# Delta rule and gated feed-forward on one core: joining the first chunk's inverses unit by unit, and the second chunk's on TensorE

## The chip, the cores and the metric

The kernel runs on one NeuronCore of a Trainium2 chip. The metric is device microseconds of one execution. Engines are named as in the profile: PE is TensorE (PEld its weight loads), DVE VectorE, ACT ScalarE, POOL GpSimd, SP the queue of SyncE that issues most transfers.

## The reference

Four batches of eight heads, 768 steps, head size 48. Per head a state S (48 x 48) is carried along the steps, with normalized keys:

```python
for t in range(S):
    y[:, :, t] = q_t @ state
    v_old = k_t @ state
    state = state + beta_t * outer(k_t, v_t - v_old)
x = y.transpose(0, 2, 1, 3).reshape(3072, 384)
h = x @ w_in                                  # 384 -> 2048
out = (h / (1 + exp(-1.702 * h))) @ w_out     # 2048 -> 384
```

The two weight matrices come as float64 and are turned into float32 on the chip.

## The kernel before

**Chunks and units.** The 768 steps are cut into six chunks of 128. A unit is one chunk of one batch with its eight heads; there are 24, in order n = 0 to 23, four to a chunk (B = 4). From chunk 1 on, a unit holds half a chunk (64 steps) of two batches (class `Half`). Within a chunk the recurrence is solved as a triangular system: the Gram matrix G of the keys, its 32 x 32 diagonal blocks inverted (`invert`, L647), and then, block by block, U = inverse x V (`solve`), with what U does to later rows subtracted from V (`below`).

**Inverting.** `invert` works on VectorE, 128 small systems side by side on the partitions, in steps that each are a multiply (P) and a reduce. It inverts the two 16 x 16 halves of every block; where the chunk is not the first, ten further pairs, five to make A = N10 x Y0 and five to make the corner from it (the loops over `(j, Q)` and `(i, Q)`), join the halves to the inverse of the 32 x 32 block. The result goes through DRAM (Yd) into XBs, where `inverse[n]` lies. For chunk 0 the join is made on TensorE by `merge` (L734): psP = G x (right columns of the inverse), scaled by `upper` on ScalarE, then psZ = inverse (transposed on VectorE) x that, added to the columns by a product with the identity. As a generator it makes psP of both units, then psZ of both.

**The start.** VectorE converts the weights by bit operations (`conversions`, six steps a piece, the second a ScalarE Relu). These steps stand in the generator `background` (L370), and `fill(us)` takes as many of them as fit an estimate; so the place of a `fill` in the program is the place of the work in VectorE's order. `background` puts the inversion of chunk 1 after the first eight pieces of w_out. TensorE's order is the program's own, since all calls are recorded in order (`pinned`). The stages:

1. Keys normalized, Gram matrices, `invert(0)`, scores of units 0 to 2.
2. The first scan, units 0 and 1: `hops` (L1455) gives eight hops that alternate between the two units, each a list of blocks to solve and a list of blocks whose U is passed on; `together` (L1289) emits one hop: head by head a solve of one unit and all updates of the other (psU, psV), then ScalarE's copies of U and of the next block's V. Between hops stand dummy products (`warm`, ps_warm), transposes of the next chunk's keys (`turn`, psT), two Gram matrices, and `fill(2.1)`. `roots_second` normalizes the next chunk's keys with a root on GpSimd; `paced` holds loads of w_in until a hop is reached.
3. `put_out` of both units: outputs psY, copied to xT, moved between partitions by transfers (xT<-last).
4. The second scan, units 2 and 3, with pieces of the first feed-forward (`feed`, ph) between hops; Gram matrices of units 6 and 7, whose diagonal blocks go by DRAM (Nd) into NT, VectorE's input for chunk 1's inversion.
5. 25 rounds of `fill(1.0)` and `feed`, in which units 8 to 11 are prepared (roots on GpSimd, rn on VectorE, KN scaled on ScalarE) and unit 4's scores are made.

**The slots** (`slot`, L1337, n = 3 to 23). Slot n solves the last block of unit n and the first of unit n + 1 (psU), makes outputs of unit n (four), updates (psR), makes scores of unit n + 2 (four again) and the Gram matrix of n + 6 (psG). Between these, `spend` takes feed-forward pieces (ph, po) from `queue`: 10.5 us of them in slots 3 to 5, 19.5 in later ones, by their estimated cost (1.3 a piece). For what is taken, `spend` also moves the inversion of the units after next along (`inverting`, from slot 4 on for units 8 and 9), and at an even slot the rest of that inversion is put out at once. `follow` adds a pair's feed-forward to the queue after each odd slot from 5 on; until then the queue holds the rest of the first two (`both_written`, `written`). When the queue is empty, `spend` does nothing.

Of the kernel before, what the change touches and what calls it, by code (L numbers as in the profile page):

```python
# [9 lines left out]
I32 = mybir.dt.int32  # L10
# [8 lines left out]
def kernel(  # L19
# [492 lines left out]
    def gram_halves(n):  # L512
# [14 lines left out]
        for t, o in evict:  # L527
# [3 lines left out]
            )  # L531
        ready[n] = KN[n % len(KN)], kT, G
        return G

# [112 lines left out]
    def invert(c, b0=0, nb=B):  # L647
# [86 lines left out]
    def merge(pair, area, banks):  # L734
# [7 lines left out]
        for X, t in zip(Z, XT):  # L742
            vec.transpose(t.rearrange("p h k -> p (h k)"), X.rearrange("p h k -> p (h k)"))
        for X, x, m in zip(pair, Z, Pm):
            ps = banks[0][0].tile([128, H, HS], F32, tag=banks[0][1], name="psP")
# [7 lines left out]
            yield  # L753
        for x, t, m in zip(Z, XT, Pm):
            ps = banks[1][0].tile([128, H, HS], F32, tag=banks[1][1], name="psZ")
            pe.matmul(ps, lhsT=ident, rhs=x[:, :, HS:], start=True, stop=True, skip_group_check=True)
            for h in range(H):
                for r in rows:
# [3 lines left out]
                    )  # L762
            act.copy(x[:, :, HS:], ps)
            yield

# [8 lines left out]
    class Step:  # L774
# [63 lines left out]
        def gather(self):  # L838
# [4 lines left out]
            )  # L843

        def below(self, blk, h, psR):
            r = slice(blk * BS, (blk + 1) * BS)
            for k in range(blk + 1, NB):
                u = slice(k * BS, (k + 1) * BS)
                pe.matmul(
                    self.psV[u, h, :], lhsT=self.G[r, h, u], rhs=self.U[r, h, :],  # L850
                    start=False, stop=True, skip_group_check=True,
                )
# [436 lines left out]
    def together(solves, belows):  # L1289
# [115 lines left out]
    for b in range(B - 1):  # L1405
# [6 lines left out]
        upper, ident.rearrange("p (k o i) -> p k o i", k=NB, o=2)[:, :, 0], axis=AX.XY, op=ALU.add  # L1412
    )
    turn(0)
    for b in range(B):
# [29 lines left out]
    warm(NY // 2)  # L1445
    scaling = roots_second(areas)
    next(scaling)

# [22 lines left out]
    scored = pair[-1].scored  # L1471
    for _ in range(HB):
        next(products)
        next(scored)
        warm(NM // 2)
    next(products)
    paced(inverse[0][0:1, 0, BS // 2 : BS // 2 + 1], 2, 1)
    fill(3.0)
    next(scaling)
    warm(NM)  # L1480
    Nds = []
    for i in range(2 * NB):
        together(*next(path))
# [3 lines left out]
        if i == 0:  # L1487
            warm(NM // 2)
            run(products)
            run(scored)  # L1490
            run(scaling)
        if i == 1:
            for X in pair[:2]:
                X.select()
        if i == 3:
            for b in range(HB, B):
# [7 lines left out]
        if i == 6:  # L1504
            Nds.append(send_blocks(B))
        if i > 5:
            fetch_out(i - 6, other_queue)
        fill(2.1 if i else 1.0)
    put_out(pair[0])
    merging = merge(pair[2:], area, ((ps_big, "big"), (ps_big, "big")))  # L1510
    fill(2.0)
    put_out(pair[1])
    Nds.append(send_blocks(B + 1))
    fetch_out(2, other_queue)
    for X in pair[2:]:
        next(merging)
        X.gather()
        warm(NM // 4)
    fill(4.0)
    for at in range(B):  # L1520
# [22 lines left out]
    for i in range(2 * NB):  # L1543
        if i == 0:
            for _ in range(HB):
                next(merging)
# [5 lines left out]
        if i == 1:  # L1552
            Nds.append(send_blocks(B + HB))
        if i == 2:
            load_diagonals(Nds + [send_blocks(B + HB + 1)])
# [104 lines left out]
```

## Time and profile before

| | us |
|---|---|
| three runs | 690.48, 691.98, 686.99 (median 690.48) |
| profiled execution | 683.09 |
| its span | 681.4 |
| busy TensorE | 660.4 (97%, dummy products included) |
| busy VectorE | 479.5 (70%) |
| busy ScalarE, GpSimd | 233.6 and 269.4 |
| mean granted clock | 0.991 |

Stages of the profiled execution, from the instructions in order of time:

| stage | us from the start |
|---|---|
| first psP (join of unit 0) | 38.7 |
| hops of the first scan | 45.5, 49.1, 51.8, 53.8, 56.1, 58.3, 60.5, 63.3 |
| last output product of unit 1 | ends 69.1 |
| first ph | 77.2 |
| second scan | 78.7 to 96.3, last psY ends 103.0 |
| chunk 1's inversion on VectorE (NT to NT) | 103.1 to 134.3 |
| po begins | 143.3 |
| slots 3, 4, 5, 6, 7 (their psU) | 153.8, 168.8, 184.4, 198.7, 224.8 |

A profile row of TensorE counts instructions; a float32 product is two. The recorded duration of a product includes its way through the array, so start times tell its pace.

### The profile page before, as it was taken

The numbers are of one execution on the slowest core, as the hardware profiler recorded it, in microseconds if no ns is written. First come the engines' busy times: TensorE is split into PE (matmuls) and PEld (weight loads), VectorE is DVE, ScalarE is ACT, GpSimd is POOL, SyncE is SP. The second block draws the span as 40 slices with busy tenths as digits, with TensorE's granted clock in tenths as the row PEclk, the third lists the DMA queues.
The fourth block names the chain that finished last, engine by engine and source line by source line (L and its number), as shares of the span: only waits on it lengthen the run. The fifth ranks groups of instructions, "written<-read, shape, count | busy, mean of one in ns | idle before, by whom it ended". The sixth has DMA issues, their size and how long they took to land.

```text
span 681.4 us, 21731 instructions
## 1 busy us (share of the span) xinstructions
PE 660.4 (97%) x9290; PEld 563.4 (83%) x9290; DVE 479.5 (70%) x890; ACT 233.6 (34%) x571; POOL 269.4 (40%) x282
## 2 busy tenths in 40 slices
PE   9899899799999999999999999999999999999997
PEld 4766678566678998998998988988988988989997
DVE  4889799983788997996997996997976970200000
ACT  2558463632333233333333233233233233322120
POOL 4032844320286634635535526426305205105041
PEclk9799999989999999999999999999999999999999
DMA  9567575263334435335335244244231130100101
GB/s 174 105 165 175 128 218 99 44 155 81 83 74 92 96 63 109 79 67 104 71 67 116 67 90 88 66 86 79 62 78 19 38 75 2 30 2 6 26 0 24
DMA packets 149632, 54.61 MB, mean 80 GB/s; under 512 B 137824, under 2 KB 142656, under 8 KB 149536
## 3 DMA queue, kind: packets, MB, share of 16 engines
q1 hardware_dynamic: 146368, 46.62, 32.7%
q0 software_dynamic: 3168, 6.61, 3.7%
q8 instruction: 73, 1.20, 0.8%
q14 instruction: 23, 0.19, 0.1%
HBM read 38.37 MB, written 13.63 MB: 76 GB/s over the span
## 4 chain that ended last, share of the span: by engine, by line
PE 86%; DVE 6%; ACT 2%; DMA 2%; issue 2%; SPq 1%; DVEq 0%; ACTq 0%
PE po L139 34%; PE ph L139 32%; PE four L139 7%; PE psU L139 3%; PE psR L139 2%; PE psG L139 2%; DVE P L139 2%; DVE w_out L139 2%; PE ps_warm L139 1%; DVE YB L139 1%; DMA TW<-in_q_dram 1%; PE psQ L139 1%; SPq L139 1%; PE psV L139 1%; DVE NT L139 1%
## 5 line engine op out<-in xcount | busy, mean ns | idle before, releaser
L139 PE MATMUL ph<-xT,w_in 128*128 128x256 f32 x1152 | 261.0, 384 | 2.3 <-ACT gT L139 2.0
L139 PEld LDWEIGHTS ph<-xT,w_in 128*128 128x128 f32 x1152 | 215.9, 190 | 33.8 <-ACT gT L139 2.4
L1118 POOL TENSOR_TENSOR gT<-gT 128x512 f32<-128x512 f32 x80 | 103.0, 1298 | 97.9 <-ACT gT L139 66.0
L139 PE MATMUL po<-w_out,gT 128*128 128x192 f32 (+1 forms) x720 | 138.4, 347 | 0.0
L139 DVE TENSOR_TENSOR P<-NT,YB 64x8 f32<-64x8 f32 (+13 forms) x195 | 124.8, 640 | 5.8
L139 PEld LDWEIGHTS po<-w_out,gT 128*128 128x128 f32 x720 | 118.5, 190 | 11.0 <-ACT o L139 0.5
L139 ACT ACTIVATE gT<-ph 128x512 f32<-128x512 f32 x90 | 53.8, 598 | 154.8 <-PE ph L139 154.8
L139 DVE TENSOR_REDUCE YB<-P 64x4 f32<-64x8 f32 (+13 forms) x195 | 78.4, 402 | 6.7
L139 PE MATMUL po<-TW,gT 128*128 128x192 f32 x480 | 81.8, 328 | 0.0
L139 PEld LDWEIGHTS po<-TW,gT 128*128 128x128 f32 x480 | 78.1, 190 | 0.7
L984 POOL TENSOR_SCALAR_AFFINE_SELECT M<-M 64x512 f32<-64x512 f32 x40 | 29.1, 727 | 90.0 <-ACT M L139 88.8
L139 DVE TENSOR_TENSOR o<-o,late 128x192 f32<-128x192 f32 x20 | 6.6, 356 | 68.1 <-ACT late L139 67.9
L139 ACT COPY VU<-psU 32x384 f32<-32x384 f32 x96 | 45.2, 470 | 21.3 <-PE psU L139 14.9
L139 DVE TENSOR_TENSOR VU<-VU,psR 32x384 f32<-32x384 f32 x40 | 22.1, 553 | 36.6 <-PE psR L139 35.9
L400 POOL TENSOR_TENSOR rn<-ssq,half 128x8 f32<-128x8 f32 x12 | 22.3, 1858 | 52.6 <-DVE ssq L139 52.6
L139 DVE TENSOR_TENSOR VU<-VU,four 128x384 f32<-128x384 f32 x19 | 10.4, 548 | 46.1 <-ACT M L139 46.0
L109 POOL DMA_DIRECT2D KN<-in_k_dram x24 | 17.2, 716 | 58.4 <-PE four L139 56.7
L139 ACT COPY o<-po 128x192 f32<-128x192 f32 (+1 forms) x44 | 14.7, 334 | 74.6 <-PE po L139 72.5
L139 PEld LDWEIGHTS psU<-VU,XBs 32*32 32x32 f32 x1536 | 27.4, 105 | 13.5 <-issue 8.5
L139 PE MATMUL psU<-VU,XBs 32*32 32x48 f32 x1536 | 32.6, 203 | 0.3 <-ACT VU L139 0.2
L139 DVE TENSOR_TENSOR P<-NT 64x512 f32<-64x512 f32 (+7 forms) x45 | 30.5, 679 | 1.1
L139 DVE TENSOR_REDUCE NT<-P 64x32 f32<-64x512 f32 (+9 forms) x45 | 30.0, 668 | 1.5
(167 smaller groups left out, 752.1 us busy)
## 6 DMA issues: line engine op xcount, KB each, us to landing
VU<-in_v_dram SPq DMA_DIRECT2D x40, 96.0 KB, 2.8
out_dram<-o SPq DMA_DIRECT2D x40, 96.0 KB, 2.2
QW<-in_q_dram SPq DMA_DIRECT2D x76, 48.0 KB, 2.2
Kd<-KN SPq DMA_DIRECT2D x56, 64.0 KB, 2.2
late<-Kd SPq DMA_DIRECT2D x14, 256.0 KB, 2.8
KN<-in_k_dram POOLq DMA_DIRECT2D x30, 96.0 KB, 3.1
w_out<-in_moe_w_out_dram SPq DMA_DIRECT2D x7, 384.0 KB, 3.8
NT<-Nd SPq DMA_DIRECT2D x20, 128.0 KB, 2.7
```

The lines of the kernel that those rows point to most:

```text
L109: dma(out=place(dst, n)[rows, :, 0:D], in_=src[b, :, t, :].rearrange("h p d -> p h d"),)
L139: return lambda *a, **kw: tc.keep_in_program_order(op(*a, **kw))
L400: nc.gpsimd.tensor_tensor(rn, ssq, half, op=ALU.pow)
L984: nc.gpsimd.affine_select(out=M, in_=M, compare_op=ALU.is_gt, fill=0.0, base=0, pattern=[[0, H], [1, CH]], channel_multiplier=-1,)
L1118: (engine or nc.gpsimd).tensor_tensor(o, a, b, op=op)
```

## The change

It has four parts.

- *The first joins.* `merge` makes psP and psZ of one unit, then of the other. The first hop follows the first unit's join. The second pair's join is spread over hops 5 to 7 of the first scan and the place after the outputs. The scores' second half, the root's continuation, the transposes and the dummy products take other places, `fill` asks for 1.9 instead of 2.1, and the Gram matrices of units 4 and 5 with the sends of all four units move from the first scan and its end into the second scan; three w_out loads on GpSimd's queue move behind the outputs.
- *The scan of units 0 to 3.* `together` emits all eight solves, the copy of U, all eight updates of the next block, the copy of V, and then the updates of the blocks further down, now one product over their joint columns.
- *Chunk 1's join.* The ten pairs on VectorE are made only for c > 1. Units 4 to 7 are joined by the new `merge_halves` with the kept Gram matrices (`grams`), the scale `minus` and an add on VectorE.
- *Where it is called.* Ahead of slot 3 for units 4 and 5 and ahead of slot 5 for units 6 and 7; at each of its five yields a piece of the queue is taken without `spend`.

```diff
     def invert(c, b0=0, nb=B):
-        if c > 0:
+        if c > 1:
             X1 = N[:, 0:HS, HS:]
...
-        for j, Q in ((0, 2), (2, 2), (4, 4), (8, 4), (12, 4)) if c > 0 else ():
+        for j, Q in ((0, 2), (2, 2), (4, 4), (8, 4), (12, 4)) if c > 1 else ():
...
-        for i, Q in ((0, 4), (4, 4), (8, 4), (12, 2), (14, 2)) if c > 0 else ():
+        for i, Q in ((0, 4), (4, 4), (8, 4), (12, 2), (14, 2)) if c > 1 else ():
...
+    def merge_halves(ns):
...
+        for X, t in zip(Z, XT):
+            vec.transpose(t.rearrange("p h k -> p (h k)"), X.rearrange("p h k -> p (h k)"))
+        yield
+        for n, x, m in zip(ns, Z, Pm):
+            ps = one_bank("psP")[:, 0 : H * HS].rearrange("p (h k) -> p h k", h=H)
+            for h in range(H):
+                for k, r in enumerate(rows):
+                    pe.matmul(
+                        ps[r, h, :], lhsT=grams[n][r, h, rows[k % 2]], rhs=x[r, h, HS:],
+                        start=True, stop=True, skip_group_check=True,
+                    )
+            act.activation(m, ps, ACT.Copy, scale=minus)
+            yield
+        for x, t, m in zip(Z, XT, Pm):
...
+                    pe.matmul(
+                        ps[r, h, :], lhsT=t[r, h, :], rhs=m[r, h, :], start=True, stop=True,
+                        skip_group_check=True,
+                    )
+            vec.tensor_tensor(x[:, :, HS:], x[:, :, HS:], ps, op=ALU.add)
             yield
...
+        def add(self, blk, h, u):
+            r = slice(blk * BS, (blk + 1) * BS)
+            pe.matmul(
+                self.psV[u, h, :], lhsT=self.G[r, h, u], rhs=self.U[r, h, :],
+                start=False, stop=True, skip_group_check=True,
+            )
+
         def below(self, blk, h, psR):
-            r = slice(blk * BS, (blk + 1) * BS)
-            for k in range(blk + 1, NB):
-                u = slice(k * BS, (k + 1) * BS)
-                pe.matmul(
...
+            self.add(blk, h, slice((blk + 1) * BS, (blk + 2) * BS))
 
         def rest(self, blk, psR):
             u = slice((blk + 1) * BS, (blk + 2) * BS)
             act.copy(self.V[u], self.psV[u])
+            if blk + 2 < NB:
+                for h in range(H):
+                    self.add(blk, h, slice((blk + 2) * BS, C))
...
     def together(solves, belows):
+        if all(X.n < B for X, blk in solves + belows):
+            for X, blk in solves:
+                for h in range(H):
+                    X.solve(blk, h, psU)
+                X.solved(blk, psU)
+            for X, blk in belows:
+                for h in range(H):
+                    X.below(blk, h, None)
+                X.rest(blk, None)
+            return
...
     for i in range(2 * NB):
         together(*next(path))
...
-        if 1 <= i <= B:
-            turn(B + i - 1)
-        if i in (5, 6):
-            gram(B + i - 5)
-        if i < 2 * NB - 1:
-            warm(NU if i == 1 else NU // 2)
...
+        if i in (3, 4):
+            turn(B + i - 3)
+            warm(NM // 2)
+        if i > 4:
+            next(merging)
+            warm(NM // 4)
+        fill(1.9)
...
     for i in range(2 * NB):
         if i == 0:
-            for _ in range(HB):
-                next(merging)
-                fill(1.0)
-            feed()
+            feed(2)
+            fill(1.5)
         together(*next(later))
-        if i < 2:
-            gram(B + HB + i)
...
+        if 1 <= i <= B:
+            gram(B + i - 1)
+        if 2 <= i <= B:
+            Nds.append(send_blocks(B + i - 2))
+        if i == B + 1:
             load_diagonals(Nds + [send_blocks(B + HB + 1)])
         feed()
         fill(2.2)
...
+    joins = {B - 1: (B, B + 1), B + 1: (B + HB, B + HB + 1)}
     for n in range(B - 1, len(units)):
+        if n in joins:
+            for _ in merge_halves(joins[n]):
+                run(take(1.3))
         slot(n, 10.5 if n < B + HB else 19.5)
```

More of the change, by code (lines that the diff above doesn't have):

```diff
@@ L532, in gram_halves @@
         ready[n] = KN[n % len(KN)], kT, G
+        if n < 2 * B:
+            grams[n] = G
         return G
@@ L743, in merge @@
             vec.transpose(t.rearrange("p h k -> p (h k)"), X.rearrange("p h k -> p (h k)"))
-        for X, x, m in zip(pair, Z, Pm):
+        for X, x, t, m in zip(pair, Z, XT, Pm):
             ps = banks[0][0].tile([128, H, HS], F32, tag=banks[0][1], name="psP")
@@ L753, in merge @@
             yield
-        for x, t, m in zip(Z, XT, Pm):
             ps = banks[1][0].tile([128, H, HS], F32, tag=banks[1][1], name="psZ")
@@ L763, in merge @@
             act.copy(x[:, :, HS:], ps)
+            yield
+    grams = {}
+    def merge_halves(ns):
+        HS = BS // 2
+        area = wk.tile([128, 3 * H * BS], F32, tag="P", name="P", bufs=1)
+        XT, Pm = (
+            [area[:, a + i * n : a + (i + 1) * n].rearrange("p (h k) -> p h k", h=H) for i in range(HB)]
+            for a, n in ((0, H * BS), (HB * H * BS, H * HS))
+        )
+        Z = [inverse[n] for n in ns]
+        rows = [slice(k * BS, (k + 1) * BS) for k in range(NB)]
+        for X, t in zip(Z, XT):
[10 more added lines that the diff above has]
+            act.activation(m, ps, ACT.Copy, scale=minus)
+            yield
+        for x, t, m in zip(Z, XT, Pm):
+            ps = one_bank("psZ")[:, 0 : H * HS].rearrange("p (h k) -> p h k", h=H)
+            for h in range(H):
+                for r in rows:
+                    pe.matmul(
[3 more added lines that the diff above has]
+            vec.tensor_tensor(x[:, :, HS:], x[:, :, HS:], ps, op=ALU.add)
             yield
@@ L843, in gather @@
             )
-        def below(self, blk, h, psR):
-            r = slice(blk * BS, (blk + 1) * BS)
-            for k in range(blk + 1, NB):
-                u = slice(k * BS, (k + 1) * BS)
-                pe.matmul(
-                    self.psV[u, h, :], lhsT=self.G[r, h, u], rhs=self.U[r, h, :],
-                    start=False, stop=True, skip_group_check=True,
-                )
+        def add(self, blk, h, u):
[3 more added lines that the diff above has]
+                start=False, stop=True, skip_group_check=True,
+            )
+        def below(self, blk, h, psR):
+            self.add(blk, h, slice((blk + 1) * BS, (blk + 2) * BS))
         def rest(self, blk, psR):
@@ L1294, in together @@
         psRs = [bank("psR") if X.n >= B else None for X, blk in belows]
+        if all(X.n < B for X, blk in solves + belows):
[4 more added lines that the diff above has]
+            for X, blk in belows:
+                for h in range(H):
+                    X.below(blk, h, None)
+                X.rest(blk, None)
+            return
         for h in range(H):
@@ L1413 @@
     )
+    minus = cpool.tile([128, 1], F32, name="minus")
+    vec.tensor_scalar(minus, upper, -1.0, None, op0=ALU.mult)
     turn(0)
@@ L1445 @@
     warm(NY // 2)
-    scaling = roots_second(areas)
-    next(scaling)
     def paced(sign, i, j):
@@ L1471 @@
     scored = pair[-1].scored
-    for _ in range(HB):
-        next(products)
-        next(scored)
-        warm(NM // 2)
+    next(products)
+    next(scored)
+    scaling = roots_second(areas)
+    next(scaling)
+    next(products)
     next(products)
     paced(inverse[0][0:1, 0, BS // 2 : BS // 2 + 1], 2, 1)
-    fill(3.0)
-    next(scaling)
-    warm(NM)
+    fill(2.0)
     Nds = []
+    slots["xT"] = wk.tile([128, 2 * DM], I32, tag="xT", name="raw", bufs=3)
+    merging = merge(pair[2:], area, ((ps_big, "big"), (ps_big, "big")))
     for i in range(2 * NB):
@@ L1487 @@
         if i == 0:
-            warm(NM // 2)
-            run(products)
+            next(products)
+            next(scored)
+        if i == 1:
             run(scored)
-            run(scaling)
-        if i == 1:
+            warm(NM // 4)
             for X in pair[:2]:
                 X.select()
+        if i == 2:
+            warm(NU // 2)
+            next(scaling)
         if i == 3:
+            run(scaling)
             for b in range(HB, B):
                 load_values(b, sync)
-        if 1 <= i <= B:
-            turn(B + i - 1)
-        if i in (5, 6):
-            gram(B + i - 5)
-        if i < 2 * NB - 1:
-            warm(NU if i == 1 else NU // 2)
[L1504 to L1508, printed above, removed]
+        if i in (3, 4):
[3 more added lines that the diff above has]
+            next(merging)
+            warm(NM // 4)
+        fill(1.9)
     put_out(pair[0])
-    merging = merge(pair[2:], area, ((ps_big, "big"), (ps_big, "big")))
     fill(2.0)
     put_out(pair[1])
-    Nds.append(send_blocks(B + 1))
-    fetch_out(2, other_queue)
+    next(merging)
     for X in pair[2:]:
-        next(merging)
         X.gather()
         warm(NM // 4)
-    fill(4.0)
+    turn(B + HB)
+    fill(3.0)
+    for f in range(3):
+        fetch_out(f, other_queue)
     for at in range(B):
@@ L1544 @@
         if i == 0:
-            for _ in range(HB):
-                next(merging)
-                fill(1.0)
-            feed()
+            feed(2)
+            fill(1.5)
         together(*next(later))
-        if i < 2:
-            gram(B + HB + i)
-        if i == 1:
-            Nds.append(send_blocks(B + HB))
-        if i == 2:
+        if i == 0:
+            turn(B + HB + 1)
+        if 1 <= i <= B:
[3 more added lines that the diff above has]
+        if i == B + 1:
             load_diagonals(Nds + [send_blocks(B + HB + 1)])
```

## The prediction

> **What bounds the kernel now.** I read the page's slices first, then busy time by stage, then the instructions in order of time of TensorE, VectorE and ScalarE up to 225 us. In the slices (a digit is a tenth of a seventeen-microsecond slice) VectorE is as full as TensorE up to the ninth:
>
> ```profile
> PE   9899899799999999999999999999999999999997
> DVE  4889799983788997996997996997976970200000
> ```
>
> Busy time by stage (span, length, then busy PE, weight load, VectorE, ScalarE, GpSimd; then the granted clock):
>
> ```profile
> 103.00:128.00 25.00, 22.72 (x137) 19.14 (x134) 23.45 (x56) 9.56 (x28) 9.90 (x11) 1.00 0.41 78
> 128.00:144.00 16.00, 12.41 (x108) 9.88 (x107) 15.20 (x32) 11.07 (x36) 6.86 (x6) 0.89 0.55 129
> ...
> 225.00:250.00 25.00, 25.00 (x458) 23.83 (x445) 23.74 (x44) 7.67 (x22) 14.63 (x13) 1.00 0.31 65
> ```
>
> From 143 us on TensorE never stops: what is added to its work there, or makes it wait, is time. Before, it waits (5.9 us in 103 to 143: 1.99, 0.30, 3.59), so VectorE's saving can count only there. So I follow TensorE's order and ask where it waits.
>
> TensorE in the first scan, before:
>
> ```profile
> 45.47 0.86 PE L139 MATMUL psU<-VU,XBs 32*32 32x48 f32 x16
> ...
> 49.08 0.23 PE L139 MATMUL psU<-VU,XBs 32*32 32x48 f32 x1
> 49.08 0.24 PE L139 MATMUL psV<-VU,gT 32*32 32x48 f32 x3
> ...
> 168.68 0.88 PE L139 MATMUL psU<-VU,XBs 32*32 32x48 f32 x64
> ```
>
> One f32 product is two instructions. 16 that all use one 32x32 square take 0.79 us in the chain of waits (0.86 with the drain); 64 on four squares take no longer, and a hop's 64, psU and psV mixed head by head, run from 49.08 to the transpose at 49.89: 0.81. So a run on one square costs 0.79 whatever its neighbours, and mixing hides three of four.
>
> **The change, part by part.**
>
> *VectorE's joins.* The ten multiply-and-reduce pairs and a copy that leave chunk 1's inversion:
>
> ```profile
> 119.43 0.96 DVE L139 TENSOR_TENSOR P<-NT,YB 128x768 f32<-128x768 f32 x1
> 120.43 0.95 DVE L139 TENSOR_REDUCE NT<-P 128x64 f32<-128x768 f32 x1
> ```
>
> are the dearest pair, 1.91; the others are 1.37, 1.19, 1.38, 0.80, 0.85, 1.38, 1.90, 1.23, 1.33 and the copy 0.39: 13.73 us.
>
> *The scans.* For the first four units all eight heads are solved first, then the next block is updated, then, after ScalarE's copy of V, the blocks further down. By the built program's waits the further update waits for that very copy. A hop is then 0.79 (solve) + 0.79 (next block), then the copies (0.47 each; U's runs beside the second run, V's ends 0.55 after it), then 0.79: 2.9 us where four hops of a scan have a further update, 1.58 in two, 0.79 in two: 16.3 us a scan. Before: 2 x 0.79 + 6 x 0.81 = 6.4. *First scan:* the first solve comes after one unit's join, at 41.6 instead of 45.5. Then per hop the 2.9, a transpose 0.5, warm-up 0.2 to 0.65 and ScalarE's conversion (0.93) ahead of the next copy make about 3.9 (before 2.2): hops at 43.9, 47.8, 51.7, 55.6, 59.6, 62.1, 64.8, outputs done at 69.3 (before 69.1). Three quarters of the second pair's join are inside it, so after that only a join, two gathers and a transpose stand before the first ph, which waits for xT (copies, 2.7 us of issue, 1.9 to land): 73.5 instead of 77.2: -3.7. This hides the lost head start; if ScalarE's copies wait longer, the bound is +1, and if only the runs count, -6. *Second scan:* before 25.8 us from first ph to last psY (77.2 to 103.0), TensorE nearly gapless, so everything counts: 16.3 - 6.4 = 9.9, two more Gram groups (0.62 each) and a transpose 0.5 moved in, 0.7 of ScalarE's queue (G 0.66, gT 0.60, conversion 0.61 stand ahead of the copies): +12.4, between 8 (half the further runs overlap) and 14. The moved block sends and the NT loads ride on SP, about 9 us of issue, and land by 96, before VectorE wants NT.
>
> [...]
>
> *25 rounds before the slots.* VectorE's last rn is 30.1 us after NT (103.06 to 133.17); in the new order it comes after 13.1 us of rows where 14.9 stood, and the part before loses 1.8: 26.5. NT itself now waits for ScalarE's conversion behind the scan's last gT: about 112.3. So rn at 138.8, the psQ that waits on it 3.7 later (as now), po 5.1 later (one ph group fewer than 6.4): 147.6. So po starts at 147.6 against 143.25: +4.4 for all before the slots; the 13.73 us save only 4.2 of the 8.7 that the scans add (bounds 2.5 and 5.9), since the program fills VectorE's place with conversions.
>
> *Joins on TensorE.* Eight groups of 32 products, each 0.66 (psP now): +5.3, all in the gapless part. Their transposes (0.38 each), adds and ScalarE's 0.37 copies lie beside a po pair or the next group (0.66).
>
> *The filler.* Each join takes five pieces of po from the queue without booking them. Slots 3, 4 and 5 had 48 products of po (18, 16, 14) and used all; with 14 taken early, slot 5 has none. It becomes a bare chain: psU 0.85, four ScalarE copies to 2.84, psR to 3.75, outputs 4.85, xT copies and the state add to 6.25, QS to 6.8, psQ 7.75, M and V to 9.0. TensorE's own work there is 4.7: +4.35 (3.5 to 5.5). The ScalarE row:
>
> ```profile
> 185.26 1.94 ACT L139 COPY VU<-psU 32x384 f32<-32x384 f32 x4 [1.61 <-PE psU L139]
> ```
>
> *Slot 7.* The inversion of units 8 and 9 is paced by filler, so slot 5 does none of it. Then slot 6 does five more pairs after psR (1.92 + 1.39 + 0.85 + 0.85 + 1.39 = 6.4):
>
> ```profile
> 217.29 1.29 DVE L139 TENSOR_TENSOR NT<-YB,bL 64x1024 f32<-64x1024 f32 x1
> ```
>
> This ends at 218.58; its way through DRAM lands 4.5 later (XBs issued 220.57, 2.3 to land), and slot 7's psU stands at 224.76: 1.7 slack. 6.4 - 1.7 = 4.7 us in which TensorE stands, po and all behind psU (0 if VectorE catches up, 8 if GpSimd's adds slow it as at 202.12). After the 3.59 us wait at 136.84 the clock was
>
> ```profile
> 137.00:138.50 1.50, 1.50 (x33) 1.22 (x29) 1.47 (x4) 0.77 (x2) 0.45 (x1) 0.50 0.87 142
> ```
>
> and psQ and the next ph took 1.73 and 2.39 for 0.93 and 1.33: +1.9 again behind this stall. [...]
>
> Sum: 4.4 + 5.3 + 4.35 + 4.7 + 1.9 = +20.6. Against the profiled execution's own 683.09 (span 681.4 and 1.7 around it) that is 703.7. That execution lies below the three timed ones (686.99 to 691.98); on their median, 690.48, it is 711.
>
> **The rivals.**
> 1. *Not slower: VectorE carries the start, and its time comes off whole.* Place: 40 to 143. Price: 13.73 and its waits there (1.41 for GpSimd's root, 0.46, 3.45 for ScalarE's w_out, 1.68): -20.7; with 16.25 in the slots, -4.5: 686. It decides where a hop stays at 2.3 us or less, so that conversions are never held. For: VectorE 19.17 of 20 in 45 to 65. Against: 16 on one square take as long as 64 on four. Should the stall of slot 7 and its clock also go, 679. Chance 0.20 (0.12 for under -1%).
> 2. *The scans as forecast, but slot 5's chain and slot 7's stall lie beside other work:* 4.4 + 5.3 = +9.7: 700. For: VectorE stood 1.26 us before psR in slot 6. Against: nothing is queued in slot 5. 0.15.
> 3. *The saving buys nothing:* rn is held by w_out loads on GpSimd's queue behind its roots: 4.2 more: 715. For: VectorE waited 1.54 for such a load at 151. 0.09.
> 4. *The scans lose the clock,* with fewer warm-ups between: half clock on 16 us, +8: 719. For: 0.50 over 21 to 27, after a wait of 1.49. Against: 1.00 in 66 to 77, with PE idle a third of it. 0.05.
> The forecast: 0.51.
>
> **How the numbers follow.** 711 is the forecast. Its own bounds: the scans and rounds 0 to +9, joins 4.6 to 5.8, slot 5 3.5 to 5.5, slot 7 3 to 9, not all at one end: 701 to 719. Down to 693 it takes in rival 2 and leaves out rival 1; up, to 719, rivals 3 and 4. A difference within 1% (683.6 to 697.4) can't be told from none. Faster 0.12; same 0.08 of rival 1 and 0.04 of rival 2: 0.12; slower 0.76.
>
> **What will show it.** In the scan psU x16 and psV x16 in runs of about 0.8 with idle ended by ScalarE's VU; hops of 3.5 to 4 us; first ph near 73.5, last psY near 112, po near 147.6. Slot 5 without po, about 9 us. A gap of 4 to 5 us before slot 7's psU, ended by the XBs load, then clock 0.50. Slots 8 to 23 and the end unchanged. If hops stay near 2.3, or VectorE has no gaps before NT, the scan step is wrong.

## The result, and the profile after

The changed kernel takes 750.1 us (median of four runs, 746.26 to 756.10) beside 690.01 before (686.99 to 691.98): a ratio of 1.088, 95% interval 1.079 to 1.098. The forecast was 711, range 693 to 719: the sign is right, the size is not. The profiled execution took 753.13 us (span 751.4), 70.0 more than the one before, where the prediction's sum was 20.6. (Ratios here and below leave out runs over 1.5% above the quickest of their kernel; medians are over all runs.)

The page after, its busy row of TensorE, VectorE's slices and the granted clock by slices of 18.8 us:

```profile
PE 713.1 (95%) x9715; PEld 610.7 (81%) x9715; DVE 467.0 (62%) x878; ACT 234.8 (31%) x575; POOL 265.8 (35%) x282
...
DVE  5864453696027569869969979699797794010000
...
PEclk9675695999999597999999999999999999999999
```

VectorE does 12.5 us less in all, which is the change's aim. But it is no longer full in the first eight slices, and TensorE's clock, 1.00 in nearly all of this before, is low in slices 2 to 5, again in slice 7, and again near 250 and 290 us. One hop of the first scan and the start of the next, on TensorE (start, duration, and in brackets the idle time before the row and what ended it):

```profile
63.84 1.24 PE L139 MATMUL psU<-VU,XBs 32*32 32x48 f32 x13
...
65.06 1.24 PE L139 MATMUL psV<-VU,gT 32*32 32x48 f32 x13
66.86 1.48 PE L139 MATMUL psV<-VU,gT 32*32 32x48 f32 x16 [0.56 <-ACT VU L139]
68.27 1.11 PE L139 MATMUL psT<-ident,KN 128*128 128x128 f32 x4
69.18 1.06 PE L139 MATMUL ps_warm<-ident 128*128 128x512 bf16 x2
70.17 1.24 PE L139 MATMUL psU<-VU,XBs 32*32 32x48 f32 x13
```

The shape is the forecast one: a run of solves, a run of next blocks, a wait ended by ScalarE's copy of V, a further run. The size is not: 6.3 us from solve to solve, against 3.9 forecast. The rows are far longer than at full clock, the transposes 1.11 for 0.66 and, from start to next start, 0.91 for 0.49. The same time by windows (length, busy PE, weight load, VectorE, ScalarE, GpSimd, then clock, DMA share, GB/s):

```profile
46.00:50.00 4.00, 4.00 (x118) 3.62 (x109) 2.85 (x5) 1.92 (x4) 2.84 (x3) 0.50 0.11 23
50.00:57.00 7.00, 6.44 (x63) 5.75 (x62) 3.18 (x6) 1.68 (x4) 2.33 (x3) 0.50 0.81 189
57.00:64.00 7.00, 6.44 (x56) 4.58 (x55) 4.66 (x7) 2.42 (x5) 0.00 (x0) 0.50 0.17 31
...
90.00:95.00 5.00, 5.00 (x116) 3.74 (x112) 2.75 (x5) 2.46 (x9) 2.62 (x5) 1.00 0.08 21
```

TensorE counts as busy for 92% of 50 to 64 us and yet was granted 0.50, from 45.6 to 90.0 us. In 50 to 64 us ScalarE waits 6.7 us for TensorE's products, and VectorE 5.4 for ScalarE, so TensorE is the bound there and all of this is time.

The second place is the join ahead of slot 5, that slot, and slot 7:

```profile
242.85 0.26 PE L139 MATMUL psZ<-P 32*32 32x16 f32 x9 [2.44 <-issue]
...
245.52 1.98 PE L139 MATMUL psR<-VU,G 32*32 32x48 f32 x32 [0.49 <-ACT VU L139]
...
251.41 1.77 PE L139 MATMUL four<-QS,kT 48*64 48x112 f32 x32 [2.00 <-ACT QS L139]
...
291.81 1.49 PE L139 MATMUL psU<-VU,XBs 32*32 32x48 f32 x60 [8.16 <-DVE P L139]
```

Slot 5 has no po: three waits, and rows twice as long as at full clock (psR 1.98 for 0.87). Slot 7 waits 8.16 us, put down to VectorE's inversion.

All profiles in one table, each stage in us: from the first psP to the first ph (first scan), to the end of the last psY (second scan), to the first po (the rounds), to slot 7's psU (the slots); then us of half clock in the two scans and in the slots. The runs are explained below.

| kernel | first scan | second scan | rounds | slots | half clock: scans | slots | median |
|---|---|---|---|---|---|---|---|
| before | 38.4 | 25.9 | 40.2 | 81.4 | 0 + 0 | 0 | 690.0 |
| after | 54.2 | 48.5 | 39.1 | 108.6 | 44 + 20 | 23 | 750.1 |
| joins_alone | 43.6 | 28.7 | 39.0 | 107.6 | 17 + 3 | 22 | 718.3 |
| scans_alone | 55.7 | 47.6 | 38.6 | 81.4 | 44 + 17 | 0 | 718.5 |
| order_undone | 43.0 | 30.0 | 39.4 | 107.6 | 34 + 0 | 21 | 719.4 |
| order_alone | 65.6 | 47.8 | 39.7 | 81.4 | 51 + 27 | 0 | 730.9 |
| runs_only | 46.8 | 28.8 | 40.3 | 81.4 | 17 + 0 | 0 | 698.9 |
| split_only | 63.0 | 44.5 | 39.7 | 81.4 | 51 + 24 | 0 | 724.6 |
| order_warmer | 54.7 | 46.5 | 38.8 | 81.4 | 20 + 17 | 0 | 725.2 |
| copy_last | 62.6 | 32.4 | 38.8 | 81.4 | 51 + 0 | 0 | 704.2 |
| after_copy_last | 52.2 | 36.3 | 38.7 | 108.0 | 41 + 0 | 21 | 737.2 |
| no_warming | 41.8 | 28.5 | 41.7 | 81.4 | 31 + 0 | 0 | 690.3 |
| first_joins | 39.2 | 29.5 | 39.0 | 81.4 | 3 + 7 | 0 | 692.9 |
| joins_booked | 44.7 | 27.8 | 40.7 | 96.3 | 17 + 0 | 7 | 704.9 |
| joins_inverting | 45.8 | 28.4 | 39.0 | 99.7 | 20 + 4 | 17 | 706.7 |
| joins_both | 44.4 | 25.9 | 40.5 | 95.3 | 17 + 0 | 3 | 703.0 |
| early_weights | 33.6 | 27.3 | 40.7 | 81.4 | 0 + 0 | 0 | 683.4 |
| after_early_weights | 53.4 | 49.8 | 39.1 | 106.6 | 44 + 24 | 21 | 749.1 |
| after_copy_last_early | 49.9 | 45.3 | 38.7 | 107.6 | 41 + 20 | 22 | 739.8 |

The two lines at the top give the 70.0: 2.6 before the first psP, 15.8 and 22.6 in the scans, -1.1 in the rounds, 27.2 in the slots, 2.9 behind slot 7 (461.3 from its psU to the end of the execution, 458.4 before). The profile of before is the most favourable line of its kernel: its granted clock was 0.991, against 0.963 to 0.989 in the other executions of before in the experiments, most of them at 0.97 to 0.98. The four profiles of joins_alone, joins_booked, joins_inverting and joins_both, whose first scan is that of before, took 43.6 to 45.8 us for it. So some 5 to 7 of the 15.8 come from the comparison and not from the change; the medians differ by 60.1. The 2.6 us belong to this one execution too: in the 15 other profiles without early loads, three of them with the changed start, the first psP stands at 37.3 to 39.2 us.

### The profile page after: what moved, and what is told of

It reads as the page before. It is cut to its first block, busy times and chain, and to the rows that moved or that the text cites. A ratio compares the mean times of both kernels' runs of the same rounds, so it can differ in the third digit from the quotient of the medians.

```text
span 751.4 us, 22578 instructions
## 1 busy us (share of the span) xinstructions
PE 713.1 (95%) x9715; PEld 610.7 (81%) x9715; DVE 467.0 (62%) x878; ACT 234.8 (31%) x575; POOL 265.8 (35%) x282
## 3 DMA queue, kind: packets, MB, share of 16 engines
q8 instruction: 76, 1.25, 0.7%
## 4 chain that ended last, share of the span: by engine, by line
PE 85%; DVE 6%; ACT 3%; issue 2%; SPq 1%; DMA 1%; POOL 0%; DVEq 0%; ACTq 0%; POOLq 0%
PE po L139 31%; PE ph L139 28%; PE four L139 7%; PE psU L139 5%; PE psV L139 3%; PE ps_warm L139 3%; PE psG L139 2%; DVE P L139 2%; PE psR L139 2%; DVE YB L139 1%; PE psQ L139 1%; PE psT L139 1%; PE psZ L139 1%; DVE NT L139 1%; ACT VU L139 1%
## 5 line engine op out<-in xcount | busy, mean ns | idle before, releaser
L139 PE MATMUL ph<-xT,w_in 128*128 128x256 f32 x1152 | 266.9, 390 | 4.6 <-ACT TW L139 3.0
L139 PEld LDWEIGHTS ph<-xT,w_in 128*128 128x128 f32 x1152 | 219.4, 194 | 38.0 <-ACT TW L139 4.0
L139 PE MATMUL po<-w_out,gT 128*128 128x192 f32 (+1 forms) x720 | 141.6, 353 | 0.0
L139 PEld LDWEIGHTS po<-w_out,gT 128*128 128x128 f32 x720 | 120.9, 193 | 10.7 <-issue 0.9
L139 DVE TENSOR_TENSOR P<-NT,YB 64x512 f32<-64x512 f32 (+23 forms) x190 | 123.4, 649 | 5.8
L139 DVE TENSOR_REDUCE YB<-P 64x2 f32<-64x2 f32 (+24 forms) x190 | 75.0, 395 | 6.5
L139 ACT COPY VU<-psU 32x384 f32<-32x384 f32 x96 | 45.0, 469 | 52.2 <-PE psU L139 51.0
L139 PEld LDWEIGHTS psU<-VU,XBs 32*32 32x32 f32 x1536 | 34.9, 116 | 22.7 <-issue 9.7
L139 PE MATMUL psU<-VU,XBs 32*32 32x48 f32 x1536 | 40.6, 217 | 8.6 <-DVE P L139 8.2
L139 DVE TENSOR_TENSOR VU<-VU,four 128x384 f32<-128x384 f32 x19 | 10.4, 550 | 47.9 <-ACT M L139 47.8
L139 DVE TENSOR_TENSOR P<-NT 64x512 f32<-64x512 f32 (+3 forms) x40 | 28.0, 699 | 1.1
L139 DVE TENSOR_REDUCE NT<-P 64x32 f32<-64x512 f32 (+4 forms) x40 | 26.7, 667 | 1.4
```

Of the source, the lines that this page charges most:

```text
L139: return lambda *a, **kw: tc.keep_in_program_order(op(*a, **kw))
```

## The experiments

**The two halves of the change.** Joins of the second chunk alone, on the kernel before, and all the rest alone.

```
joins_alone: before with
-        if c > 0:
+        if c > 1:
...
+        if n in joins:
+            for _ in merge_halves(joins[n]):
+                run(take(1.3))
scans_alone: after without these lines
```

> Before, with only the second chunk's joins moved to TensorE (the scans, first joins and Gram work as before). Theory: the joins take the products that the slots would have had, so slot 5 runs bare and at a low clock, VectorE's inversion for units 8 and 9 is late, and slot 7 waits 8 us for it: the stages from slot 3 on cost as in the changed kernel, +25 to +32 us over the kernel before, less the 6.6 us of output products that are only pulled forward and up to 4 us that VectorE saves in the rounds: +15 to +25. Rival A, the prediction's own sizes (joins 5.3, bare slot 5 4.35, slot 7 4.7, clock 1.9, rounds -4.2): +12. Rival B, the late slots of the changed kernel are only a consequence of its late start (the output products begin 40 us later): +5 or less.

> The changed kernel with the second chunk's join left on VectorE as before (new first joins, new hops, moved Gram work and warming products stay). Theory: the scans' half clock carries the larger part of the loss, the start of the first output product is again about 40 us later: +35 to +45 over the kernel before. Rival A (the prediction's sizes: first scan -3.7, second +12.4, no saving in the rounds): +9. Rival B (the scans' loss is made good later, VectorE having been the slower one in the rounds): under +20, and the changed kernel's loss would lie in the joins.

Joins alone: 718.29, ratio 1.041 (1.036 to 1.047): +28.4, a little over the theory's range, and its slots are those of the changed kernel (107.6 and 108.6 us). The rest alone: 718.45, 1.040 (1.033 to 1.047): +28.6, where +35 to +45 was expected. The two add up to 57 of the 60 us, so both halves are losses of their own. In the rounds, joins_alone gains 1.1 us: what leaves VectorE saves almost nothing.

**The order of the hops.** Undone in the changed kernel, and alone in the kernel before.

```
-        if all(X.n < B for X, blk in solves + belows):
-            for X, blk in solves:
...
-            return
order_undone: after without this branch, and with the old below and rest
order_alone: before with the branch and the new below and rest
```

> The changed kernel with the hops' products in the order of before (one unit's solve and the other's block products head by head in turn, all lower blocks before the copy of V). Theory that the serial order on one 32x32 square is what drops TensorE's clock: the granted clock is 0.9 or more through the first scan, the first output product starts 20 to 35 us earlier than in the changed kernel, and the time is 20 to 35 us below it. Rival (the warming products that went are what held the clock): the clock still falls to half in the first scan, and the time is at most 10 us below the changed kernel.

> Before, with only the hops' order changed (a unit's solve in one run, then the other's next block, the copy of V, then its further blocks); warming products, Gram work, first joins and the second chunk's join as before. Theory that the serial order drops the clock: clock near 0.5 in both scans, +25 to +40 us over the kernel before. Rival A (the warming products held the clock): the clock stays at 0.9 or more in the first scan, and the hops cost only their longer chain, some 1 us each or less: 0 to +12 us, half of it in the second scan, which has no warming products. Rival B (the order costs nothing by itself): within 3 us.

Undone: 719.37, 30.7 less than the changed kernel and equal to joins_alone, so the moved Gram groups, sends and warming products together cost nothing that is seen beside it. Its clock did fall, to half from 42.4 to 76.6 us, which the theory had not expected; yet its first scan took 43.0 us, against 54.2 in the changed kernel. Alone: 730.93, 1.058 (1.052 to 1.065), +41: more than in the changed kernel. The order of the hops is the whole loss of the scans.

**Which half of the order.** Runs instead of head by head (runs_only), or further blocks behind the copy of V (split_only).

```
runs_only: before with the branch in together; below and rest as before
split_only: before with the new below and rest, together as before:
             act.copy(self.V[u], self.psV[u])
+            if blk + 2 < NB:
+                for h in range(H):
+                    self.add(blk, h, slice((blk + 2) * BS, C))
```

> Before, with only one half of the new hop order: a unit's 16 solve products in one run, then the other unit's block products (all lower blocks, before the copy of V, as before). Separates the two halves of the +41 us that the whole order cost alone. Theory that runs on one 32x32 square let the clock fall: half clock in most of both scans and +20 us or more over the kernel before. Rival, that the further blocks behind the copy of V (a wait of 0.56 us and 16 more products in each hop) carry it: +5 us or less here, and most of the 41 in the other half.

> Before, with only the other half of the new hop order: solve and next block interleaved head by head as before, but the further blocks' products only after the copy of V. Theory that runs on one square drop the clock: +5 to +12 us (8 such waits and runs more, at full clock 0.56 + 0.8 us each, = 11 at most, the clock held). Rival, that the wait on the copy and the run behind it carry the loss: +20 us or more and the clock near half in both scans.

My theory was wrong here. Runs on one square cost +12.6 (698.89; ratio 1.020, 1.007 to 1.033), between the two expectations; the further blocks behind the copy cost +38.3 (724.59; 1.057, 1.052 to 1.062). Split_only's second scan, in windows of 3.4 us set on the clock's changes:

```profile
101.70:105.10 3.40, 3.40 (x58) 2.77 (x57) 2.79 (x6) 1.12 (x3) 3.40 (x7) 1.00 0.59 92
105.10:108.50 3.40, 2.17 (x50) 1.70 (x49) 1.70 (x5) 1.92 (x4) 2.99 (x6) 1.00 0.82 248
108.50:111.90 3.40, 3.40 (x41) 2.83 (x40) 2.03 (x3) 1.16 (x3) 3.40 (x4) 0.50 0.58 151
111.90:115.30 3.40, 2.42 (x51) 1.90 (x50) 1.77 (x4) 0.84 (x2) 3.40 (x7) 1.00 0.81 160
115.30:118.70 3.40, 3.40 (x24) 2.40 (x26) 0.00 (x0) 0.58 (x2) 2.13 (x4) 0.50 0.95 250
118.70:122.10 3.40, 2.30 (x42) 1.99 (x38) 2.71 (x6) 2.07 (x5) 0.00 (x0) 1.00 0.96 364
122.10:125.50 3.40, 2.42 (x36) 1.58 (x35) 1.65 (x4) 0.84 (x2) 0.99 (x1) 0.51 0.44 150
```

A window of 2.2 to 2.4 us busy, with a wait of about 1 us in it, is followed by one at half clock, a full one by one at full clock. That holds in this stretch; another below goes against it. runs_only has no such wait, and once its clock is back it stays:

```profile
64.00:68.00 4.00, 4.00 (x105) 3.31 (x103) 3.46 (x6) 2.86 (x6) 0.36 (x1) 1.00 0.32 97
68.00:72.00 4.00, 4.00 (x82) 2.77 (x81) 2.88 (x6) 3.05 (x7) 1.53 (x3) 1.00 0.79 147
```

**Without the wait.** The further blocks go ahead of the copy: the same products, no wait of TensorE in the hop.

```
+            if blk + 2 < NB:
+                for h in range(H):
+                    self.add(blk, h, slice((blk + 2) * BS, C))
             act.copy(self.V[u], self.psV[u])
-            if blk + 2 < NB:
-                for h in range(H):
-                    self.add(blk, h, slice((blk + 2) * BS, C))
copy_last: in order_alone; after_copy_last: in after
```

> Before with the whole new hop order, but a hop's further block products are put ahead of the copy of V instead of behind it: the same products in the same runs, and TensorE no longer waits for ScalarE's copy in the middle of a hop (0.56 us, 0.98 to 1.23 us with interleaved solves). The copy itself comes about 1 us later. Theory that this wait is what keeps the clock at half: 695 to 707 us (with runs on one square alone it was 698.9), the clock 0.9 or more after 65 us. Rival, that the further run of 16 products by itself is what is too much: 720 us or more, as with the copy first (730.9).

> The changed kernel with the same single edit: further block products ahead of the copy of V. Theory that the wait behind the copy carries most of what the scans lose: 20 to 30 us below the changed kernel, 720 to 730 us, as with the whole order undone (719.4). Rival A, that it needs the warming products too, which this kernel has few of: 735 to 745. Rival B, that the wait does nothing: within 6 us of 750.

copy_last: 704.15, 26.8 less than order_alone (ratio to before 1.008, 1.002 to 1.014). Its ten executions go with the clock that each was granted: 690.2 us at 0.994, 694.1 to 695.3 at 0.987 to 0.988, 703.7 to 706.3 at 0.966 to 0.973, 711.6 to 713.8 at 0.954 to 0.956; the profile is one of the last. One and the same program thus differs by up to 24 us as its clock does. With the clock all but whole, the new order without the wait costs about 7 us (690.2, against 683.3 for the quickest execution of before in that round, at 0.989). after_copy_last: 737.23, 12.9 less than the changed kernel; rival A's numbers. Both have their second scan at 1.00 throughout, and it falls from 47.8 to 32.4 and from 48.5 to 36.3 us. The first scan stays at half in both profiles. So taking the wait away gave the second scan its clock back in these two profiles, and was not enough in the first scan. It does not always do it: after_copy_last_early below has no such wait either, and its second scan took 45.3 us, 20 of them at half clock, behind windows without a gap (the profile is of the slowest of its four executions, 744.2 us at a granted clock of 0.929; the others had 0.938 to 0.946):

```profile
97.60:101.00 3.40, 3.40 (x80) 2.92 (x81) 3.33 (x8) 1.47 (x4) 2.92 (x5) 1.00 0.49 161
101.00:104.40 3.40, 3.40 (x29) 2.27 (x21) 1.24 (x2) 0.94 (x4) 3.35 (x6) 0.50 0.26 35
```

**What holds the clock in the first scan.** More warming products in every hop, and none.

```
order_warmer: order_alone with
             act.copy(self.V[u], self.psV[u])
+            warm(NU // 2)
no_warming: before without
-            warm(NM // 2)
...
-        if i < 2 * NB - 1:
-            warm(NU if i == 1 else NU // 2)
```

> Before with the whole new hop order (730.9 us alone), and three more 128x512 bf16 products in every hop, put behind the copy of V, where TensorE waits 0.56 us: work added and nothing taken away. Theory that the serial hops are slow because the clock falls, not because of their chain: the clock goes back to 0.9 or more in the scans and the time falls by 15 to 30 us to 700 to 716. Rival, that the chain of small products is what is long: each of 14 hops gets 0.25 to 0.9 us longer, 734 to 743 us, the clock whatever it is.

> Before without the 26 warming products (128x512 bf16) in the hops of the first scan; nothing else is changed, and they are no part of the result. Theory that full-array products hold the clock there: once the clock has fallen at the stall near 42 us it doesn't come back in the first scan, 5 to 15 us slower than before. Rival, that TensorE's mere busy time holds it: 26 products of some 0.25 us are saved, 0 to 6 us faster.

order_warmer: 725.19, 5.7 less than order_alone and not the 15 to 30 expected. Its four executions again go with the granted clock: 708.9 us at 0.980, 718.2 at 0.966, 732.1 at 0.945 and 737.8 at 0.937, beside 726.7 to 731.7 at 0.934 to 0.943 in order_alone. So the added products cost some us where the clock stays as low, and the clock that they bring back in some executions gains more. Its first scan is back at 1.00 from 63.5 us, and its last four hops take 4.1, 4.1, 3.5 and 3.4 us; in order_alone, at half clock, they take 6.8, 6.7, 4.9 and 4.8. no_warming: 690.30, ratio 0.998 (0.995 to 1.001): its clock stays at half up to 74.5 us, as the theory said, instead of 59 to 61 in joins_alone, joins_inverting and joins_both, whose first scan is that of before; but the time is unchanged (the rival's outcome): in the old order the products save about what they cost. Six of its hops, at half clock and without these products, took 2.4 to 2.6 us, those of order_undone at half clock 2.8 to 3.8, the first left out; before, at full clock and with them, 2.0 to 2.3. The new order's hops with further blocks took 6.2 to 6.6 at half clock in the changed kernel. So half clock costs the old order little in the first scan, and the new one much: it takes both to make the loss. The six hops of no_warming:

```profile
54.30:69.40 15.10, 15.01 (x368) 12.59 (x368) 10.35 (x15) 10.88 (x22) 4.59 (x7) 0.50 0.64 141
```

**The idle time near 42 us.** In every profile but that of before and the three with early loads, the clock falls at 42.4 to 45.6 us, in an idle stretch of TensorE or just behind it. In order_alone:

```profile
41.11 0.71 PE L139 MATMUL psQ<-TW,kT 48*128 48x128 f32 x7
45.03 0.58 PE L139 MATMUL psQ<-TW,kT 48*128 48x128 f32 x1 [3.21 <-issue]
```

The row names nothing that it waits for. It is 1.8 to 3.6 us long in these, and was 1.0 in the profile of before, which the prediction was built on. It ends 1 to 3 us behind a burst that fills all DMA engines (in order_alone, their busy share is 0.97 to 1.15 in each half microsecond from 38.8 to 42.3 us, at 180 to 238 GB/s).

The packets in the traces go with it. In the changed kernel's page one of the queues (packets, MB, share) is

```profile
q8 instruction: 76, 1.25, 0.7%
```

Its packets are of 16 KB each (1.25 MB in 76), and the page counts 19430 instructions on PE and PEld, 255.7 to a packet. My estimate from these counts is 256 instructions of TensorE to a packet, 19456 in all. The 19 profiles have 61 idle stretches of TensorE over 0.5 us that end in "issue". All of them stand where TensorE's records number 193 more than a multiple of 256 (1217 at this place, or 1473), and all end 1.2 to 1.8 us after a packet of q8 has landed: in order_alone it travels from 42.28 to 43.56, and TensorE goes on at 45.03. By these counts I take it that TensorE waits here for its own instructions. In the 16 profiles without early loads this packet starts 1.3 to 3.5 us after TensorE has begun on the 256 before it, while the burst runs; the next packet, with the burst over, starts after 1.0 to 1.2. The loads of w_in's second quarter, moved out of the burst:

```
     for b in range(B - 1):
         load(b, ((QP, q),), sync)
+    fetch_in(1)
     warm(NW)
...
-    fetch_in(1)
early_weights: in before; after_early_weights: in after
after_copy_last_early: in after_copy_last
```

> Before with one group of loads (the second quarter of the first weight matrix, 12 transfers, about 1.2 MB) issued at the start of the queue instead of behind the keys and values, so that the transfers that fill all DMA engines from 29 to 42 us end earlier. Theory that TensorE's unexplained idle time at 41 to 45 us (1.0 to 3.6 us in 14 profiles, ending 1 to 2 us behind the end of that burst) hangs on the burst, and that the clock's fall there is what makes 690 of 683: the idle time is at most 1 us, the clock stays at 1.00 from 28 to 100 us, and the time is 3 to 8 us under the kernel before. Rival, that it is a fixed cost of that place in the program: the same idle time, within 2 us of before.

> The changed kernel with the same loads issued earlier. Theory that the new order of the hops drops the clock by itself (in the whole order alone it rose at 63.9 us and fell again at 67.3): at most 8 us below the changed kernel, 742 to 750, the clock still at half in most of the first scan. Rival, that the idle time at 43 us is the trigger and the first scan would hold the clock without it: 15 to 22 us below, 728 to 735.

> The changed kernel with both edits: further block products ahead of the copy of V (737.2 us alone) and the second quarter's loads issued early (749.1 us alone). Theory that the first scan is held at half by either of two things, the idle time near 43 us and the wait on the copy of V, so that each edit alone leaves it there: with both the clock is 0.9 or more from 45 to 90 us and the time is 716 to 726 us. Rival, that runs of 16 products on one square with few warming products between them drop it by themselves in that scan: the clock falls again soon after 45 us, 732 to 740.

early_weights: 683.43 (683.11 to 690.93) beside 691.36, ratio 0.990 (0.987 to 0.994): 1% faster than before. The packet of instructions lands at 41.78, ahead of its use, the idle time is gone, the same rows now follow each other, and the clock stays at 1.00 from 36.1 to 121.5 us:

```profile
43.99 0.72 PE L139 MATMUL psQ<-TW,kT 48*128 48x128 f32 x8
44.64 0.61 PE L139 MATMUL ps_warm<-ident 128*128 128x512 bf16 x2
```

after_early_weights: 749.07, nothing gained. There is no idle stretch at 43 us, only one of 1.26 from 46.3, and the clock falls 0.3 us into it, at 46.6, and stays down to 91.0. after_copy_last_early: 739.75, the rival's numbers: with no copy wait either, the clock falls at 46.4, 0.2 us into an idle stretch of 1.16 and behind more than 3.4 us without a gap, and is back at 87.4. So in the first scan the changed kernel loses the clock without the long stretch at 43 us and keeps it lost without the wait on the copy. Its runs of small products with fewer warming products between them are what is left to blame; no run tests that by itself.

**The first joins** alone (a unit's psZ right behind its psP):

```
-        for X, x, m in zip(pair, Z, Pm):
+        for X, x, t, m in zip(pair, Z, XT, Pm):
...
-        for x, t, m in zip(Z, XT, Pm):
```

> Before with only the first part of the change: in both early joins a unit's second product group comes right behind its first instead of behind the other unit's. Theory that this part costs or saves next to nothing (the second group waits for ScalarE's copy of the first, 0.37 us in the profile, once per unit): within 4 us of the kernel before. Rival, that it starts the first scan earlier by the join that is no longer ahead of it, as the prediction had it (3.7 us earlier to the first product of the second stage): 2 to 4 us faster.

692.92, ratio 1.002 (0.9995 to 1.005): no effect that can be told, as the theory said.

**The joins' 28 us.** Two repairs on joins_alone: products that a join takes are subtracted from the next slot's share (joins_booked), and the inversion goes on where no product paces it (joins_inverting); then both.

```
joins_booked:
+                for done_ in take(1.3):
+                    share -= done_
+                    due[0] += 0.72 * done_
...
joins_inverting, in spend:
+        if not queue:
+            due[0] += rate * cost
+            while due[0] > 0:
+                due[0] -= next(inverting, 1e9)
```

> Before with the second chunk's joins on TensorE (718.3 us alone), but the output products that a join takes between its steps are subtracted from the share of the slot behind it, and VectorE's inversion advances by them as it does in a slot. Theory that the joins cost by the empty queue in slot 5 and the late inversion: slot 5 has its products again, the inversion for units 8 and 9 no longer ends 8 us late before slot 7, and the time is 695 to 704 us (before + 5 to 14, the joins' 5.3 us and a part of the rest). Rival, that the joins' own products, turns and waits cost it: within 6 us of 718.

> Before with the second chunk's joins on TensorE (718.3 us alone), and VectorE's inversion goes on by its share in a slot also where no output products are left to pace it (slot 5). Theory that slot 7's wait of 8.3 us is the late inversion: the wait is gone or under 2 us, 709 to 713 us, and slot 5 stays bare (its 5 us of waits and the half clock behind them stay). Rival, that the wait only changes its place (the inversion's work now delays slot 5's own VectorE steps): within 4 us of 718.

> Before with the second chunk's joins on TensorE, with both repairs: the products taken in a join are subtracted from the next slot's share (704.9 us), and VectorE's inversion goes on where no products are left (706.7 us). Theory that what is left is the joins' own 5.3 us and the waits of slots with fewer products: 697 to 704 us, that is before + 6 to 13. Rival, that both repairs mend the same loss: 704 to 707.

Booked: 704.94, just above the expected 695 to 704. Slot 7's wait is gone and the half clock is 7 us instead of 22, but 5.1 us of waits are left, at other places, the longest now the join itself, which comes too close to its slot:

```profile
207.99 0.88 PE L139 MATMUL psU<-VU,XBs 32*32 32x48 f32 x64 [1.78 <-DVE XBs L139]
```

Inverting: 706.67, below the expected 709 to 713. Slot 7's 8.3 us are gone (slots 99.7 for 107.6), slot 5 stays bare. Both: 702.99, ratio 1.014 (1.009 to 1.019): inside the theory's 697 to 704, but only 2 to 4 below one repair, so the two do mend mostly the same loss. What is left in the slots, 95.3 against 81.4, is 5.2 of joins, 5.1 of waits, and 3.6 more, mostly po rows (45.8 us for 43.0); 3.4 us of the slots were at half clock.

## Why the prediction was wrong

The marks along the way came late: first ph at 95.6 us (forecast 73.5), last psY at 144.1 (112), po at 183.2 (147.6). Term by term:

- **First scan, -3.7:** measured +18.4 (2.6 before the first psP, 15.8 after). The hop was put at 3.9 us; it took 6.3 at half clock. Where the new order did run at full clock (order_warmer), hops took 3.4 to 4.4, three more warming products included. This step failed: it took full clock as given, from a profile in which it happened to hold. The old order stood half clock with 2.4 to 3.8 us a hop (no_warming, order_undone), so the loss is the clock times the longer hop: three runs in a row, 1.2 to 1.9 us each for the 0.79 forecast, stand where one was.
- **Second scan, +12.4:** measured +22.6. At full clock and without the copy wait it is +10.4 (after_copy_last 36.3 against 25.9); the wait adds 2.4 (four times 0.56, and 0.16). Its working was right for full clock; some 10 us are missing from it, with 20 us of half clock. Rival 4 had this mechanism, and priced it at 8 us for both scans, with a chance of 0.05.
- **Rounds, -4.2:** measured -1.1 (by the prediction's own 8.7 less 4.4 it should have said 4.3). The rounds take 38.6 to 41.7 us in all 19 profiles, with the join on VectorE or without. Waits for ScalarE (in joins_both 2.39 on gT and 2.15 on QS, before 1.99 and 3.59) still stand where they stood. Rival 3's outcome, though no load on GpSimd's queue was shown to be its cause; rival 1, VectorE carrying the start, is ruled out.
- **Joins on TensorE, +5.3:** the psP and psZ groups took 5.3, right.
- **Bare slot 5, +4.35:** 5.5 us of waits, 2.44 of them the unforeseen "issue" in the join, where TensorE waited for instructions (the packet landed at 241.49, TensorE went on at 242.85).
- **Slot 7, +4.7:** 8.2; joins_inverting shows that the late inversion is its cause. The five further pairs behind psR came as forecast. What was not foreseen is that psR itself came later: slot 6 ran at half clock up to 260.6 us, psR came 12.2 us behind psU (9.4 before), and VectorE stood 5.27 us for it with those pairs still to do.
- **Half clock behind the stall, +1.9:** the 27.2 us of the slots less 5.3, 5.5 and 8.2 leave 8.2 for rows that ran longer, over 23 us of half clock, 17 of them from 243.6 to 260.6 us in slots 5 and 6, where none was forecast. The waits of slot 5 stand in that stretch: the clock fell 0.7 us behind the one of 2.44, and stayed down through those of 0.49 and 2.00. In split_only the changes at 108.5, 111.9, 115.3, 118.7 and 122.1 us lie 3.4 us apart. TensorE didn't have to be idle for all of such a window to lose the clock: 2.2 to 2.4 us busy of 3.4 was not enough to keep it in split_only, nor 3.4 of 3.4 in after_copy_last_early.
- **Behind slot 7, 0:** measured +2.9, the half clock up to 298.2 us.

What stays open: what the clock counts. Before, windows of 3.41 us, as long as its stretch at 0.50 from 136.93 to 140.34, with 2.2 to 2.8 us busy kept 1.00 (65 to 79 us, with psY and psV products of 128 rows among them), while in order_alone one of 3.40 with 2.84 us busy, mostly on 32x32 products, lost it (63.9 to 67.3), in after_copy_last_early full ones lost it, and in the changed kernel full windows from 77.9 to 88.2 us stayed at 0.50. So busy time alone doesn't decide in these windows. Whether the kind of product counts, no run measured by itself. No profile shows the changed first scan at full clock as a whole either, so its 18.4 us can't be divided exactly into clock and longer chain.

## What to carry to other kernels

Before adding a wait or a run of small products to a chain on TensorE, price it at half clock too, and see in more than one execution whether the clock is only just held: one favourable profile hid that here. In split_only, about 1 us of waiting in 3.4 was followed by 3.4 to 17 us at a clock of 0.50. Count small products in packets of instructions as well: 64 matmul instructions with their 64 weight loads ran in 0.66 us here, so that by my estimate a packet of 256 lasts 1.3. In the changed kernel's last join TensorE began on a packet at 238.96 us, and the next one landed at 241.49. Work taken off an engine that is full saved only 1.1 of 13.7 us here, since TensorE's waits for ScalarE (2.39 and 2.15 us in joins_both) stood where they were; and work that takes filler from a queue must give it back to whoever was paced by it. Doing each half of a change alone, and again each half of that half, found the costliest line, a copy put ahead of products that don't need it.

## What the runs showed of the hardware

- The granted clock was 0.50 or 1.00 in these profiles, and its changes lie a whole number of times 3.4 us apart: in the changed kernel it is 0.50 from 110.44 us, 1.00 from 124.10, 0.50 from 127.51 and 1.00 from 134.34 (13.66, 3.41 and 6.83 us), in split_only five changes follow each other at 3.4 us (windows above).
- TensorE was busy without a gap and yet stayed at 0.50 for long: order_warmer from 44.2 to 63.0 us, 18.8 us busy of 18.8.
- A window of 3.4 us without a gap, at 1.00, was followed by one at 0.50 (after_copy_last_early, 97.6 to 101.0 us).
- TensorE idled where, by the counts above, its next 256 instructions arrived late: 61 of 61 idle stretches marked "issue" (0.5 to 3.6 us) end 1.2 to 1.8 us after a 16 KB packet of q8 lands (the eight in the profiles of before and after: 1.35 to 1.59 us). They stand near 20 us, near 42 us, ahead of the second scan and in it, and at joins, most of them behind runs of small products. The one near 42 us is gone when 12 loads leave the DMA burst ahead of it (early_weights); the one of 2.44 us in the last join or slot 5 stands where no po products lie between (after, joins_inverting) and is gone where they do (joins_booked, joins_both).
